# Attention and gated MLP on one core: q and k stacks moved per head, one transfer for the reciprocals, pairs ordered at the score buffers, another start order

## The chip, the cores and the metric

The kernel runs on one core of a Trainium2 chip. The metric is device time in microseconds of one launch. Three runs of the kernel before gave 1013.47, 1013.8 and 1016.6, so the median is 1013.8 us. The profile comes from a separate execution of 1009.12 us, whose span from first to last instruction is 1007.3 us.

## The reference, cut to what matters

```
q, k, v: 8 batches x 8 heads x 576 positions x 64
q, k = rotate(q), rotate(k)              # rotary embedding, x*cos + swapped(x)*sin
attn = softmax(q k^T / 8), 576 x 576     # max subtracted, sum + 1e-9
x    = attn v, heads side by side        # 8 x 576 x 512
h    = relu(x w_in)                      # 512 -> 1024, halves u and v
v_n  = (v - mean) / sqrt(var + 1e-6)
v_s  = w_spatial v_n + b_spatial         # mixes the 576 positions
out  = (u * v_s) w_out                   # 512 -> 512
```

All arithmetic is to float32 accuracy. A matmul operand is split into a rounded high part and a low rest, and products of parts are summed: three matmuls per product in the MLP; in the scores the high and the low half of a factor are stacked on the 128 rows, so two matmuls do.

## The kernel before, in words

**Pairs and batches.** The unit of attention is a pair of heads; there are 4 pairs per batch and 32 in all. After the four pairs of a batch comes that batch's MLP.

**One pair.** `prepare(i)` (L440) loads q and k into two stage buffers `st` (three slots), multiplies by the rotation tables and adds (L485, L489, mostly GpSimd), rounds the high parts (`hq` by L368, high k in the second half of `st[1]` by L501) and takes the rests (`lq` L371, `lk` L469). Eleven DMAs on SP's queue then build the operands of the score matmuls: `ks` (4: each head's high k at its own rows and at the other head's rows), `qs` (2 from `hq`, 2 from `lq`) and `qz` (3). `qs`, `ks`, `qz`, `hq` and `lq` exist once each, and `lk` has one slot. So the stacks of pair i+1 may be written only when the scores of pair i have been read out of them.

**Scores.** `scores` (L551) runs nine times per pair, in the order `TILES` = 0, 1, 2, 3, 8, 4, 5, 6, 7: tiles 0 to 3 are head 0, tiles 4 to 7 head 1, tile 8 (fifth in order) holds the last 64 rows of both heads. Each is 4 or 6 matmuls into a score buffer (`sc`, two in PSUM), a row maximum on VectorE (L571), an exponential on ScalarE (L572) into `e` (three slots) and a transpose on VectorE (L582) into `tu` (one slot). `need` (L569) makes every tile wait for all stacks of both heads.

**Values.** `attention` (L523) then multiplies the transposed tiles with v (L541): 288 small matmuls, in three chunks, into two `pm` buffers and one of the two `sc` buffers. `normalise` (L586) inverts the sums (L621, L622), transposes them into `rt` (L623), writes them to a scratch in DRAM by four DMAs (`put`), reads them back spread over the partitions by three (`get`, into `rb`), and multiplies the values by them (L618, L619). Only then is the value accumulators' PSUM, the `sc` buffer among it, free.

**The MLP.** Four products: L660 (v half of h), L683 (u half), L701 (spatial) and L721 / L738 (output), 360 matmuls per batch. Its weights arrive as 64-bit floats and are decoded at the start (`decode`, L376): twelve pieces of 512 KB, each six VectorE and two ScalarE instructions.

**What sets the order.** Every instruction group is an `op` with an estimated duration and a key. `Program.run` (L138) plays the program with these estimates: an engine that is free takes the ready op with the lowest key whose buffers are free. The order that comes out is written into the instruction queues, and each queue runs in that order on the chip, waiting where an estimate was too short. The DMAs of `load` (L365) and `unroll` (L350 to L352) all stand in SP's one queue. Until 100 us of planned time, idle TensorE slots are filled with matmuls on zeros (L795).

Of the kernel before, what the change touches and what calls it, by code (L numbers as in the profile page):

```python
# [8 lines left out]
F32 = mybir.dt.float32  # L9
# [7 lines left out]
P = 128  # L17
# [7 lines left out]
HALF = S // 2  # L25
# [6 lines left out]
TO_PE = 105  # L32
IBUF, BLOCK, FETCH = 544, 256, 3900
SLOTS = {
    "stage": 3, "lk": 1, "vraw": 1, "e": 3, "tu": 1, "rb": 1, "x32": 1, "xg": 7, "m": 4,
    "small": 3, "nmx": 3, "rt": 2, "sc": 2, "pm": 4,
}
PSUM = {"sc": 1024, "pm": 512}
MOE_START, MOE_LENGTH = 163.72, 41.17
DEC_V = [-3.48, -27.9, 65.72, -23.46]  # L40
DEC_S = [83.89, 51.11, 39.65]
DEC_U = [-100.9, 67.61, 53.75, 139.76]
DEC_ON = -44.85
DEC_O = [-11.86, 63.73, 86.56, 156.33]

NB = S // 32
TILES = [0, 1, 2, 3, 8, 4, 5, 6, 7]
NV = 4 * NQ
JC = 4 * P + 16
Q4 = S // 4  # L50
CHUNKS = 3
QE = JC + P
EARLY = 73.59
STEAL = 145.22
WARM_FROM, WARM_FULL, WARM_TO, WARM_NS, WARM_AFTER, WARM_COLS = 2500, 44958.22, 100000, 170, -0.15, 384
PATIENT = (DVE, ACT, POOL)
UNTIL = 144.95
LATE_LOAD = 2200
FIRST = 6
PREP = [-17.58, -1.0, 26.46, -6.17, -39.31, -66.56, -25.92, 107.58]  # L60
PREP_E = [114.39, 49.39, -30.17, 40.83, 35.03, -30.24, -3.45, 80.62]
PREP_AT = [37.74, 27.86, 33.62, 20.81, 13.42, 36.67]
STAGE = [-22.63, 3.68, -25.96, -10.67, -21.35, 14.58, 46.93]
STAGE_E = [-7.1, 1.79, 3.9, 176.64, 8.86, -89.19, 11.72]
ATT_AT = [-190.38, 50.74, 48.75, -18.56, -25.99, -28.18]
NORM = [-24.83, -11.6, 65.82, 18.85, 38.51]
NORM_E = [92.6, -206.08, -98.79, -5.14, -12.64]
MOE0 = [281.73, 20.17]
K_NORM, K_RELU, K_GATE, K_GHI, K_GLO, K_OB, K_OUT = 158.97, -96.57, 62.21, 63.93, -95.55, -267.44, -2.21


def pe_ns(n, m=P):
    return max(m * 5 // 6 + 3, n * 11 // 24)
# [33 lines left out]
class Program:  # L107
# [5 lines left out]
    def op(self, eng, ns, key, f, r=(), w=(), new=(), port=False, late=0):  # L113
        return self.either({eng: ns}, key, lambda e: f(), r, w, new, port, late)
# [23 lines left out]
    def run(self, make, warm):  # L138
# [34 lines left out]
        while events:  # L173
# [29 lines left out]
            for e in LATENCY:  # L203
# [17 lines left out]
                        kept = kept or len(item[2].new) == 3  # L221
                if chosen and e in PATIENT:
                    soon[e] = {a for a in soon[e] if not a.eng and a.due > now}
                    if any(a.key < min(chosen.key, UNTIL) and a.due < now + chosen.costs[e] * 0.5 for a in soon[e]):
                        for b in chosen.new:
                            free[b.pool].insert(0, b.slot)
                            own[b.pools[0]] += 1
                        passed.append(item)
                        chosen = None
                for item in passed:  # L230
                    heapq.heappush(ready[e], item)
                if e == PE and not chosen and max(WARM_FROM, idle + (WARM_AFTER if now > WARM_FULL else 0)) <= now < WARM_TO and free["pm"]:
                    chosen = warm()
                    chosen.bufs[0].pool, chosen.bufs[0].slot = "pm", free["pm"].pop(0)
                    index[chosen] = len(index)
                    left += 1
# [36 lines left out]
def tile_attention_gated_mlp(  # L273
# [24 lines left out]
    def make(b):  # L298
        tag = f"{b.pool}{b.slot}"
        if b.pool in PSUM:  # L300
            return ps.tile([P, PSUM[b.pool]], F32, tag=tag, name=b.name, bufs=1)
        if b.pool == "rt":
            b.scratch = dr.tile([9, P], F32, tag=tag, name=b.name + "d", bufs=1)
        return sb.tile(b.shape, b.dt, tag=tag, name=b.name, bufs=1)

    prog = Program()
# [47 lines left out]
    def at(t, offset, *dims):  # L354

        return bass.AP(tensor=t.tensor, offset=t.offset + offset, ap=[list(d) for d in dims])
# [7 lines left out]
    def load(dst, src):  # L364
        nc.sync.dma_start(out=dst, in_=src)  # L365
# [10 lines left out]
    def decode(key, where, at, src):  # L376
# [26 lines left out]
            return lambda: ts(out=ints(), in0=word(1), scalar1=s1, scalar2=s2, op0=op0, op1=op1)  # L403

        t0, t1 = (tok, 0), (tok, 1)
        op(DMA, 1500, key - 8, fetch, w=[t0, t1])
        op(DVE, 640, key, bits(20, 0x7FF, ALU.logical_shift_right, ALU.bitwise_and), r=[t1], w=[pt], new=[pt])
        op(ACT, 600, key - DEC_ON, lambda: nc.scalar.activation(ints(), ints(), AF.Relu, bias=bias, scale=float(2**23)), r=["bias"], w=[pt])
        op(DVE, 640, key - DEC_ON, lambda: stt(out=sg.tile, in0=word(1), scalar=-(2**31), in1=ints(), op0=ALU.bitwise_and, op1=ALU.bitwise_or), r=[t1, pt], w=[sg], new=[sg])
# [5 lines left out]

    def spatial(key, j):
        st = Buf("xg", [P, 2, S], F32, f"ws{j}")
        op(DMA, 1700, key - 8, lambda: load(st.tile, w_spT[j * P:(j + 2) * P, :].rearrange("(c p) t -> p c t", p=P)), w=[st], new=[st])
        for c in range(2):
            t = ("wsp", j + c)  # L420
            op(ACT, 573, key, lambda c=c: round_hi(wsp[:, j + c, 0, :], st[:, c, :]), r=[st], w=[(t, 0)])
            pair_op(S, key, lambda e, c=c: rest_lo(e, wsp[:, j + c, 1, :], st[:, c, :], wsp[:, j + c, 0, :]), r=[st, (t, 0)], w=[t])
# [17 lines left out]
    def prepare(i):  # L440
# [60 lines left out]
        op(ACT, 573, key - K_HIQ, lambda: nc.scalar.activation(hk(), st[1][:, :S], AF.Copy, scale=0.125), r=[(st[1], 0)], w=[(st[1], 1)])  # L501
        op(DVE, dve_ns(S), key - K_LOK, lo_k, port=True, r=[(st[1], 0), (st[1], 1)], w=[lk], new=[lk])

        def stack(dst, src, swap):
            for a in range(2):
                rows = slice(64 * a, 64 * a + 64)
                to = slice(64 - 64 * a, P - 64 * a) if swap else rows
                load(raw(dst[to, a, :]), raw(src[rows, :]))

        def to_z():  # L510
            load(raw(qz[0:64, :QE]), raw(hq[0:64, :]))
            load(raw(qz[64:P, JC:QE]), raw(hq[64:P, 4 * P:JC + P - 16]))
            load(raw(qz[64:P, QE:]), raw(hq[64:P, :4 * P]))

        op(DMA, 1250, key - K_STACK, lambda: stack(qs, hq, False), r=["hq"], w=[("qs", 0)])
        op(DMA, 1250, key - K_STACK, lambda: stack(ks, hk(), False), r=[(st[1], 1)], w=[("ks", 0)])
        op(DMA, 1250, key - K_STACK2, lambda: stack(ks, hk(), True), r=[(st[1], 1)], w=[("ks", 1)])
        op(DMA, 1850, key - K_STACK, to_z, r=["hq"], w=["qz"])
        op(DMA, 1250, key - K_STACK2, lambda: stack(qs, lq, True), r=["lq"], w=[("qs", 1)])

    raw = lambda t: t.bitcast(F32)

    def attention(i):  # L523
        lk, vr = prepped[i]
        sm = sums[i % 2]
        key = 20 * i
        K_S, K_STEP, K_MAX, K_EXP, K_TURN, K_CHUNK, K_VAL = STAGE_E if i < FIRST else STAGE
        if i < FIRST:
            key += ATT_AT[i]
        tu = Buf("tu", [P, NB, HALF], F32, f"tu{i}")  # L530
        for n, c in enumerate(TILES):
            scores(i, c, lk, sm, key + K_S + K_STEP * n, K_MAX, K_EXP, K_TURN, tu, n == 0)
        pv = [*[Buf("pm", None, None, f"pv{i}_{g}") for g in range(2)], Buf("sc", None, None, f"pv{i}_2")]

        def values(n):
            outs = [pv[0][:, :Q4], pv[1][:, :Q4], pv[2][:, :Q4], pv[2][:, 512:512 + Q4]]
            for kb in range(NB * n // CHUNKS, NB * (n + 1) // CHUNKS):
                for a in range(2):
                    for g in range(4):
                        rows = slice(32 * g, 32 * g + 32)  # L540
                        nc.tensor.matmul(outs[g][64 * a:64 * a + 64], lhsT=vr[rows, NQ * (kb % 4) + kb // 4, a, :], rhs=tu[rows, kb, Q4 * a:Q4 * a + Q4], start=(kb == 0), stop=(kb == NB - 1), tile_position=(32 * g, 64 * a))  # L541

        for n in range(CHUNKS):
            o = op(PE, NB * 243 // CHUNKS + 200, key + K_VAL + K_CHUNK * n, lambda n=n: values(n), r=[vr, *[(tu, c) for c in TILES]], w=pv, new=pv if n == 0 else [])
            o.words = NB * 32 // CHUNKS
        normalise(i, sm, pv, key)

# [3 lines left out]
    def scores(i, c, lk, sm, key, k_max, k_exp, k_turn, tu, first):  # L551
# [14 lines left out]
                for n_c in range(2):  # L566
                    nc.tensor.matmul(pt[:, n_c * 512:n_c * 512 + HALF], lhsT=lhsT, rhs=rhs[:, n_c * HALF:n_c * HALF + HALF], start=(n == 0), stop=(n == len(parts) - 1))  # L567

        need = [lk, ("qs", 0), ("qs", 1), ("ks", 0), ("ks", 1), "qz"]  # L569
        op(PE, (6 if c == 8 else 4) * pe_ns(HALF), key, mm, r=need, w=[pt], new=[pt])  # L570
        op(DVE, 749, key + k_max, lambda: nc.vector.tensor_reduce(out=nmx.tile, in_=tops(pt), op=ALU.max, axis=AX.XY, negate=True), r=[pt], w=[nmx], new=[nmx])  # L571
        op(ACT, 920, key + k_exp, lambda: nc.scalar.activation(e.tile.rearrange("p (c n) -> p c n", c=2), tops(pt), AF.Exp, bias=nmx.tile, scale=1.0, accum_out=sm[:, col:col + 1]), r=[pt, nmx], w=[e, ("sums", i % 2, c)], new=[e])  # L572

# [12 lines left out]
    def normalise(i, sm, pv, key):  # L586
# [6 lines left out]
        need = [("sums", i % 2, c) for c in range(9)]  # L593

        def put():
            for g in range(4):
                load(at(rt.scratch, 9 * 32 * g, (32, 9), (1, 32)), rt[32 * g:32 * g + 9, :])

        def get():
            load(rb[0:64], at(rt.scratch, 0, (0, 64), (9 * 32, 4), (1, Q4)))  # L600
            load(rb[64:P, :, :P], at(rt.scratch, P + 32, (0, 64), (9 * 32, 4), (1, P)))
            load(rb[64:P, :, P:], at(rt.scratch, Q4, (0, 64), (9 * 32, 4), (1, 16)))

        def low(e):
            rest_lo(e, four(x[:, S + TW:S + TW + 4 * P]), x32[:, :, :P], four(x[:, :4 * P]))
# [15 lines left out]
        op(ACT, 100, key + K_INV, lambda: nc.scalar.activation(sm[:, 0:9], sm[:, 0:9], AF.Copy, bias=1e-9), w=need)  # L621
        op(DVE, 130, key + K_INV, lambda: nc.vector.reciprocal(out=sm[:, 0:9], in_=sm[:, 0:9]), w=need)  # L622
        op(DVE, 125, key + K_INV, lambda: nc.vector.transpose(out=rt.tile, in_=sm), r=need, w=[rt], new=[rt])  # L623
        op(DMA, 1500, key + K_INV, put, r=[rt], w=[(rt, 1)], late=2000)
        op(DMA, 1850, key + K_GET, get, r=[(rt, 1)], w=[rb], new=[rb], late=1000)
        op(DVE, dve_ns(S) + 220, key + K_X, scale, r=[*pv, rb], w=[x32], new=[x32])
        op(ACT, 660, key + K_XHI, high, r=[x32, *([("gated", i // NP - 1)] if i >= NP and i % NP == NP - 1 else [])], w=[(x, 0)], new=[x])
# [172 lines left out]
    pairs = [(b, hp) for b in range(B) for hp in range(NP)]  # L800
    prepped, xs = [], []
    n_setup = [("sums", n, c) for n in range(2) for c in range(9)]
    n_setup += [("qs", 0), ("qs", 1), "qz", "hq", "lq"]
    op(POOL, 2000, -126, setup, w=["bias", *n_setup])

    def tables():
# [85 lines left out]
```

## Time and profile before

| | |
|---|---|
| median of three runs | 1013.8 us |
| profiled execution | 1009.12 us |
| its span | 1007.3 us |
| mean granted TensorE clock | 0.944 of full speed |
| TensorE busy | 894.8 us (89%), of which 74.8 us on zeros |
| VectorE / ScalarE / GpSimd busy | 608.8 / 490.8 / 482.9 us |
| moved by DMA | 160.78 MB, mean 160 GB/s |

Busy shares are averages over a start (weights are loaded and decoded, no MLP yet), a long middle (attention of one batch beside the MLP of the batch before) and an end (the last MLP alone). TensorE's busy time counts modelled matmul ends and matmuls at the low clock, so it is more than the work would take at full speed.

### The profile page before, as it was taken

Reading aid. Unit: us, or ns where it says so; the run is one execution under the profiler, and the core shown is the slowest. Engines: PE = TensorE matmul, PEld = TensorE weight load, DVE = VectorE, ACT = ScalarE, POOL = GpSimd, SP = SyncE. Lnnn points to the kernel's source line nnn. Section 1 sums busy time; section 2 is a strip of 40 time slices with the busy share of each in tenths; the row PEclk is TensorE's granted clock in tenths of the full one; section 3 lists DMA queues with packets and bytes.
Section 4 is the critical chain, followed back from the end, with each engine's and each line's share of the span. In section 5 each row is a group of like instructions: output and inputs, shape, how many; then the busy total and the mean of one; then the engine's idle time right before and its main releaser. Section 6 shows DMA issues by size and latency. Waiting matters only on the chain.

```text
span 1007.3 us, 32514 instructions
## 1 busy us (share of the span) xinstructions
PE 894.8 (89%) x13677; PEld 784.3 (78%) x13677; DVE 608.8 (60%) x1202; ACT 490.8 (49%) x1207; POOL 482.9 (48%) x468
## 2 busy tenths in 40 slices
PE   8779856989898999989799997998899987999998
PEld 4456645788788887888778986887779886898898
DVE  3888865645677654745576665655576645765331
ACT  1454433644456543654456453753456443663352
POOL 3554344454555561845356654545356651742022
PEclk9789957989999999999989997999989998999999
DMA  9976666755777668766686677775676667855101
GB/s 242 258 210 182 156 146 130 176 145 131 168 199 162 159 153 212 179 157 152 165 190 152 159 199 164 168 169 138 172 179 141 164 167 184 192 130 124 62 1 48
DMA packets 99380, 160.78 MB, mean 160 GB/s; under 512 B 26849, under 2 KB 45665, under 8 KB 99234
## 3 DMA queue, kind: packets, MB, share of 16 engines
q1 hardware_dynamic: 98578, 157.45, 64.8%
q8 instruction: 108, 1.77, 0.8%
q10 hardware_dynamic: 656, 1.25, 0.5%
q14 instruction: 38, 0.31, 0.1%
HBM read 98.08 MB, written 9.58 MB: 107 GB/s over the span
## 4 chain that ended last, share of the span: by engine, by line
PE 40%; SPq 10%; DMA 6%; issue 4%; DVE 4%; POOL 2%; ACT 2%; DVEq 0%; POOLq 0%
PE sc L567 9%; SPq L365 7%; PE pc L701 7%; PE pb L683 7%; PE pd L721 6%; PE pv L541 6%; PE pa L660 5%; DMA st<-in_qk_dram 2%; POOL st L485 1%; DVE tu L582 1%; SPq L352 1%; SPq L351 1%; POOL st L489 1%; DMA ks<-st 1%; SPq L350 1%
## 5 line engine op out<-in xcount | busy, mean ns | idle before, releaser
L571 DVE TENSOR_REDUCE nmx<-sc 128x1 f32<-128x576 f32 x288 | 212.8, 747 | 197.6 <-PE sc L567 194.8
L572 ACT ACTIVATE e<-sc,nmx 128x576 f32<-128x576 f32 x288 | 212.7, 740 | 172.8 <-DVE nmx L571 170.8
L582 DVE STREAM_TRANSPOSE tu<-e 128x576 f32<-128x576 f32 x288 | 219.0, 767 | 42.8 <-ACT e L572 33.4
L485 POOL TENSOR_TENSOR st<-st,tabs 128x576 f32<-128x576 f32 x124 | 175.0, 1433 | 109.2 <-DMA st<-in_qk_dram 102.7
L541 PE MATMUL pv<-tu,vr 32*64 32x144 f32 x9216 | 187.7, 294 | 33.6 <-issue 20.4
L567 PE MATMUL sc<-ks,qs 128*128 128x288 f32 x640 | 153.2, 332 | 62.1 <-ACT e L572 30.4
L541 PEld LDWEIGHTS pv<-tu,vr 32*64 32x64 f32 x9216 | 155.7, 134 | 61.8 <-issue 43.5
L567 PEld LDWEIGHTS sc<-ks,qs 128*128 128x128 f32 x640 | 110.7, 205 | 85.4 <-ACT e L572 38.1
L567 PE MATMUL sc<-lk,qz 128*128 128x288 f32 x576 | 132.3, 313 | 0.0
L371 POOL TENSOR_TENSOR lq<-st,hq 128x512 fp32r<-128x512 f32 (+1 forms) x62 | 48.5, 807 | 169.8 <-ACT hq L368 168.0
L660 PE MATMUL pa<-wi,x 128*128 128x512 f32 x448 | 122.4, 410 | 0.1
L701 PE MATMUL pc<-wsp,vn 128*128 128x288 f32 x768 | 121.7, 297 | 0.0
L683 PE MATMUL pb<-x,wi 128*128 128x288 f32 x768 | 115.8, 296 | 0.3 <-ACT vv L759 0.3
L721 PE MATMUL pd<-g,wo 128*128 128x288 f32 x744 | 113.5, 300 | 0.0
L683 PEld LDWEIGHTS pb<-x,wi 128*128 128x128 f32 x768 | 106.6, 188 | 4.7 <-issue 1.8
L701 PEld LDWEIGHTS pc<-wsp,vn 128*128 128x128 f32 x768 | 108.0, 188 | 2.8 <-issue 2.8
L721 PEld LDWEIGHTS pd<-g,wo 128*128 128x128 f32 x744 | 104.7, 192 | 1.8 <-issue 1.8
L567 PEld LDWEIGHTS sc<-lk,qz 128*128 128x128 f32 x576 | 100.9, 205 | 0.1
L660 PEld LDWEIGHTS pa<-wi,x 128*128 128x128 f32 x448 | 83.0, 196 | 17.6 <-issue 3.7
L489 POOL TENSOR_TENSOR st<-st 128x576 f32<-128x576 f32 x62 | 89.2, 1439 | 4.9 <-DVE st L485 2.0
L371 POOL TENSOR_TENSOR x<-x,x 128x64 fp32r<-128x64 f32 (+1 forms) x96 | 59.3, 647 | 67.1 <-ACT x L368 67.1
L795 PE MATMUL warm<-zero 128*128 128x384 bf16 x365 | 74.8, 348 | 13.0 <-DVE wi L371 10.1
(104 smaller groups left out, 772.4 us busy)
## 6 DMA issues: line engine op xcount, KB each, us to landing
vr<-in_v_dram SPq DMA_DIRECT2D x128, 320.0 KB
st<-in_qk_dram SPq DMA_DIRECT2D x32, 576.0 KB
ks<-st SPq DMA_DIRECT2D x128, 144.0 KB
qs<-lq SPq DMA_DIRECT2D x64, 164.0 KB
qs<-hq SPq DMA_DIRECT2D x64, 164.0 KB
st<-in_qk_dram SPq DMA_DIRECT2D x32, 288.0 KB
out_dram<-ob SPq DMA_DIRECT2D x31, 288.0 KB
st<-in_qk_dram SPq DMA_DIRECT2D x32, 256.0 KB
```

The lines of the kernel that those rows point to most:

```text
L371: eng.tensor_tensor(out=lo, in0=src, in1=hi.bitcast(F32), op=ALU.subtract)
L485: f = lambda e: e.tensor_tensor(out=st[j][:, cols], in0=st[j][:, cols], in1=tabs[j][:, cols], op=ALU.mult)
L489: f = lambda e: e.tensor_tensor(out=st[j][:, :S], in0=st[j][:, :S], in1=st[j][:, S:2 * S], op=ALU.add)
L541: nc.tensor.matmul(outs[g][64 * a:64 * a + 64], lhsT=vr[rows, NQ * (kb % 4) + kb // 4, a, :], rhs=tu[rows, kb, Q4 * a:Q4 * a + Q4], start= ...
L567: nc.tensor.matmul(pt[:, n_c * 512:n_c * 512 + HALF], lhsT=lhsT, rhs=rhs[:, n_c * HALF:n_c * HALF + HALF], start=(n == 0), stop=(n == len( ...
L571: op(DVE, 749, key + k_max, lambda: nc.vector.tensor_reduce(out=nmx.tile, in_=tops(pt), op=ALU.max, axis=AX.XY, negate=True), r=[pt], w=[n ...
L572: op(ACT, 920, key + k_exp, lambda: nc.scalar.activation(e.tile.rearrange("p (c n) -> p c n", c=2), tops(pt), AF.Exp, bias=nmx.tile, scale ...
L582: nc.vector.transpose(out=dst, in_=src)
L660: nc.tensor.matmul(pm[:, :HF], lhsT=lhsT, rhs=win[1, d][:, j, :], start=(d == 0 and n == 0), stop=(d == 3 and n == len(todo) - 1))
L683: nc.tensor.matmul(pm[:, :HALF], lhsT=win[0, d][:, i, f * P:(f + 1) * P], rhs=x[d][:, at:at + HALF], start=(d == 0 and n == 0), stop=(d == ...
L701: nc.tensor.matmul(pm[:, :HALF], lhsT=lhsT, rhs=rhs, start=(t == 0 and n == 0), stop=(t == 4 and n == 1))
L721: nc.tensor.matmul(pm[:, :HALF], lhsT=wout[d,][:, i, m * P:(m + 1) * P], rhs=gs[d][:, at:at + HALF], start=(d == 0 and n == 0), stop=(d == ...
```

## The change

The moves of the stacks are grouped by head rather than by operand. The same eleven DMAs are issued, but the tokens are per head (`("ks", a)`, `("qs", a, 0)`, `("qs", a, 1)`, `("qz", a)`), and a score tile waits only for the stacks of the heads that it reads. `lk` gets a second slot.

Two ordering tokens are added for the planner. `("all", i - 1)`: no score tile of pair i is placed before the last of pair i-1. `("go", i - 1)`: tiles after the fourth of pair i are not placed before the first value chunk of pair i-1. Zero matmuls are not placed while values wait for their buffers.

`put` becomes one DMA of the whole 128x32 tile, into a scratch of that shape, and `get` reads it with the matching strides.

The estimated durations of some DMAs change (weight pieces 1500 to 2200, spatial loads 1700 to 2300, `put` 1500 to 600), and nearly all keys change: the order of the decoding, the keys of `prepare`, `scores`, `normalise` and the MLP. `UNTIL` and the factor `SOON` change when VectorE, ScalarE and GpSimd hold back for a more urgent op.

```diff
-    "stage": 3, "lk": 1, "vraw": 1, "e": 3, "tu": 1, "rb": 1, "x32": 1, "xg": 7, "m": 4,
+    "stage": 3, "lk": 2, "vraw": 1, "e": 3, "tu": 1, "rb": 1, "x32": 1, "xg": 7, "m": 4,
-MOE_START, MOE_LENGTH = 163.72, 41.17
-DEC_V = [-3.48, -27.9, 65.72, -23.46]
-DEC_S = [83.89, 51.11, 39.65]
-DEC_U = [-100.9, 67.61, 53.75, 139.76]
+MOE_START, MOE_LENGTH = 92.6, 82.21
+DEC_V = [-26.92, 52.32, 24.86, 22.99]
+DEC_S = [150.62, 151.46, 121.54]
+DEC_U = [13.26, 87.85, 110.17, 61.84]
-PREP_E = [114.39, 49.39, -30.17, 40.83, 35.03, -30.24, -3.45, 80.62]
-PREP_AT = [37.74, 27.86, 33.62, 20.81, 13.42, 36.67]
-STAGE = [-22.63, 3.68, -25.96, -10.67, -21.35, 14.58, 46.93]
+PREP_E = [56.57, 104.31, -2.68, 90.22, 41.0, 15.18, 35.33, 70.53]
+PREP_AT = [-49.94, 1.99, -17.86, 1.88, 5.93, 3.81]
+STAGE = [-8.68, 1.44, -30.59, -19.57, 31.94, 1.12, 13.88]
-MOE0 = [281.73, 20.17]
+MOE0 = [84.13, 114.68]
...
-            b.scratch = dr.tile([9, P], F32, tag=tag, name=b.name + "d", bufs=1)
+            b.scratch = dr.tile([P, 32], F32, tag=tag, name=b.name + "d", bufs=1)
...
-        op(DMA, 1250, key - K_STACK, lambda: stack(qs, hq, False), r=["hq"], w=[("qs", 0)])
-        op(DMA, 1250, key - K_STACK, lambda: stack(ks, hk(), False), r=[(st[1], 1)], w=[("ks", 0)])
-        op(DMA, 1250, key - K_STACK2, lambda: stack(ks, hk(), True), r=[(st[1], 1)], w=[("ks", 1)])
-        op(DMA, 1850, key - K_STACK, to_z, r=["hq"], w=["qz"])
-        op(DMA, 1250, key - K_STACK2, lambda: stack(qs, lq, True), r=["lq"], w=[("qs", 1)])
+        def high_q(a):
+            own, _ = half(a)
+            load(raw(qs[own, a, :]), raw(hq[own]))
+            if a == 0:
+                load(raw(qz[own, :QE]), raw(hq[own]))
+            else:
+                load(raw(qz[own, JC:QE]), raw(hq[own, 4 * P:JC + P - 16]))
+                load(raw(qz[own, QE:]), raw(hq[own, :4 * P]))
+
+        def high_k(a):
+            own, other = half(a)
+            load(raw(ks[own, a, :]), raw(hk(own)))
+            load(raw(ks[other, a, :]), raw(hk(own)))
+
+        def low_q(a):
+            own, other = half(a)
+            load(raw(qs[other, a, :]), raw(lq[own]))
+
+        for a in range(2):
+            late = K_LATE * a
+            op(DMA, 1250, key - K_STACK + late, lambda a=a: high_k(a), r=[(st[1], 1)], w=[("ks", a)])
+            op(DMA, 1250 + 600 * a, key - K_STACK + late, lambda a=a: high_q(a), r=["hq"], w=[("qs", a, 0), ("qz", a)])
+            op(DMA, 650, key - K_STACK2 + late, lambda a=a: low_q(a), r=["lq"], w=[("qs", a, 1)])
...
-            o = op(PE, NB * 243 // CHUNKS + 200, key + K_VAL + K_CHUNK * n, lambda n=n: values(n), r=[vr, *[(tu, c) for c in TILES]], w=pv, new=pv if n == 0 else [])
+            o = op(PE, NB * 243 // CHUNKS + 200, key + K_VAL + K_CHUNK * n, lambda n=n: values(n), r=[vr, *[(tu, c) for c in TILES]], w=[*pv, *[("go", i)][:1 - n]], new=pv if n == 0 else [])
...
-        need = [lk, ("qs", 0), ("qs", 1), ("ks", 0), ("ks", 1), "qz"]
-        op(PE, (6 if c == 8 else 4) * pe_ns(HALF), key, mm, r=need, w=[pt], new=[pt])
+        need = [lk, *[t for a in heads for t in (("qs", a, 0), ("qs", a, 1), ("ks", a), ("qz", a))]]
+        op(PE, (6 if c == 8 else 4) * pe_ns(HALF), key, mm, r=[*need, ("all", i - 1), *([("go", i - 1)] if TILES.index(c) > SLOTS["e"] else [])], w=[pt, *([("all", i)] if c == TILES[-1] else [])], new=[pt])
...
         def put():
-            for g in range(4):
-                load(at(rt.scratch, 9 * 32 * g, (32, 9), (1, 32)), rt[32 * g:32 * g + 9, :])
+            load(rt.scratch, rt.tile)
```

## Rows read from the trace of the kernel before

**Rows 1.** Stages: stretch, length, busy PE, PEld, DVE, ACT, POOL; clock, DMA share, GB/s.
```profile
43.60:170.40 126.80, 95.88 (x1535) 70.69 (x1535) 93.23 (x151) 53.54 (x123) 57.59 (x54) 0.83 0.73 183
294.40:941.00 646.60, 590.71 (x9616) 537.36 (x9615) 400.44 (x814) 338.49 (x850) 330.87 (x317) 0.96 0.69 163
```

**Rows 2.** Sums turned for the reciprocals, once per pair: first and last start.
```profile
L623 DVE STREAM_TRANSPOSE rt<-sums x32: 169/204/214, 59.4 to 941.1; 128x32 f32<-128x32 f32 x32
...
L365 SPq DMA_DIRECT2D rt3d<-rt x4: 304/310/450, 151.6 to 152.8; - x4
```

**Rows 3.** SP's queue in time: start us, us, operation, count. Stacks of pair 19.
```profile
565.03 7.80 SPq L365 DMA_DIRECT2D ks<-st  x2
...
576.78 1.54 SPq L365 DMA_DIRECT2D rt18d<-rt  x4
578.37 2.21 SPq L365 DMA_DIRECT2D qz<-hq  x3
...
583.91 1.91 SPq L365 DMA_DIRECT2D rb<-rt18d  x3
```

**Rows 4.** TensorE in time, same stretch: last tile of pair 18, tiles of 19.
```profile
572.14 0.43 PE L567 MATMUL sc<-lk,qz 128*128 128x288 f32 x2
...
583.49 0.53 PE L567 MATMUL sc<-ks,qs 128*128 128x288 f32 x2
...
586.13 0.43 PE L567 MATMUL sc<-ks,qs 128*128 128x288 f32 x2
...
599.05 0.43 PE L567 MATMUL sc<-lk,qz 128*128 128x288 f32 x2
```

**Rows 5.** VectorE in time, pair 18: last transpose and its normalisation.
```profile
575.24 0.78 DVE L582 STREAM_TRANSPOSE tu<-e 128x576 f32<-128x576 f32 x1
...
587.91 0.52 DVE L618 TENSOR_TENSOR x<-pv,rb 128x144 f32<-128x144 f32 x2 [0.30 <-DMA rb<-rt18d]
```

**Rows 6.** Who SP's queue waited for: us in total, times, longest.
```profile
SPq L365 <- PE sc L567: 272.7, 55, 7.5
```

**Rows 7.** Pieces of the chain that ended last: start us, us, what.
```profile
564.73 1.33 PE sc L567 x10
...
941.63 1.71 PE pv L541 x96
...
950.36 11.74 PE pa L660 x50
...
964.69 10.53 PE pb L683 x78
...
977.60 13.69 PE pc L701 x103
991.29 9.18 PE pd L721 x69
```

**Rows 8.** Idle time of TensorE, whole span: line, releaser, us, times, longest.
```profile
PEld pv L541 <- issue: 43.5, 97, 2.1
...
PE pv L541 <- issue: 20.4, 23, 1.9
```

**Rows 9.** Idle time of TensorE from 170 to 950 us, same columns.
```profile
PE sc L567 <- DVE x L619: 23.7, 15, 3.1
```

**Rows 10.** SP's queue at the start: pair 0's first and last stack moves.
```profile
19.28 1.90 SPq L365 DMA_DIRECT2D ks<-st  x2
...
36.77 1.75 SPq L365 DMA_DIRECT2D qz<-hq  x3
```

**Rows 11.** TensorE in time: the first score matmul.
```profile
43.61 0.51 PE L567 MATMUL sc<-ks,qs 128*128 128x288 f32 x2
```

**Rows 12.** Costly groups: busy us, mean ns of one, idle before.
```profile
L571 DVE TENSOR_REDUCE nmx<-sc 128x1 f32<-128x576 f32 x288 | 212.8, 747 | 197.6 <-PE sc L567 194.8
L582 DVE STREAM_TRANSPOSE tu<-e 128x576 f32<-128x576 f32 x288 | 219.0, 767 | 42.8 <-ACT e L572 33.4 <-PE pv L541 8.3
...
L412 DVE SCALAR_TENSOR_TENSOR dcwi<-dcwi,sgwi 128x512 f32<-128x512 f32 x8 | 5.6, 696 | 0.2
```

## What the change was expected to do

> **What bounds the kernel now.** I read the busy time by stages first. In the middle, TensorE is busy 590.7 of 646.6 us at 0.96 of full clock [rows 1], which looks like an engine near its limit. The length of a pair says otherwise. The sums of a pair are turned once per pair, from 59.4 to 941.1 us [rows 2]: 31 periods of 28.4 us; those up to pair 3 take 30.7 us each, when no MLP runs yet, the 28 after it 28.2 us. A period that is the longer without the MLP's work is no TensorE limit.
>
> What TensorE needs per pair, at full clock, comes from pieces of the last chain [rows 7]. Scores: 38 matmuls at 0.133 us = 5.05. Values: 288 at 1.71/96 = 0.0178 us = 5.13. MLP per batch: 56 at 11.74/50 = 0.235, 96 at 10.53/78 = 0.135, 112 at 13.69/103 and 96 at 9.18/69 = 0.133: 53.8 us, so 13.4 per pair. Together 23.6 us, 4.6 less than the period.
>
> The ring is seen in SP's queue and TensorE read side by side. Pair 18's last score matmul ends at 572.57 [rows 4]. Only then can SP issue the stacks of pair 19: its `ks` entry ends at 572.83 after a wait, the last `qz` is issued at 580.58, with four puts of 1.54 us in between [rows 3]. The first score of pair 19 starts at 583.49 and its last ends at 599.48 [rows 4]. So a period is a gap of 10.9 us (8.0 of issues, 2.9 until the last has landed) and a score stage of 16.0 us (1.78 per tile). SP waits 272.7 us in all for score matmuls [rows 6], 8.8 per pair. In the gap TensorE has values and MLP work, but the gap makes the MLP of a batch run out before the next batch's inputs are there, and this is where idle time and low clock come from.
>
> **The change part by part.** *Stacks by head.* The eleven DMAs stay, at (8.0 - 1.54)/11 = 0.59 us of issue each. Head 0's five can go once the fifth tile of the pair before has been computed: 2.9 us of issue and 2.9 of landing, 5.8 us, beside four head-1 tiles that take 4 x 1.78 = 7.1 us. They are hidden, with 1.3 us to spare. Head 1's six need 3.5 + 2.9 = 6.4 us after the last tile; the first tile that wants them is the fifth of the next pair, behind four head-0 tiles and a value chunk. Hidden too. If that cover fails, the fifth tile waits up to the old gap. `lk`'s second slot adds no instruction; without it the next pair could not start beside the old one.
>
> What is late next is the ring through `tu`, of one slot. After the last transpose ends (576.02, [rows 5]) the values run until 583.49 [rows 4]: 7.5 us with MLP matmuls in between. Three tiles of the next pair can wait in the three `e` slots; six remain: 6 x 1.78 = 10.7 us. From the last score to the last transpose it is 576.02 - 572.57 = 3.45 us. Sum 21.6 us. Lower end: values alone 3 x 1.71 = 5.1 [rows 7], tiles at VectorE's own pace, 0.747 + 0.767 = 1.51 us [rows 12]: 5.1 + 9.1 + 3.45 = 17.7. Upper end: no tile runs ahead, 7.5 + 16.0 + 3.45 = 27.0. I take 21.6, as the code now lets three tiles through ahead of the values.
>
> So TensorE becomes the bound: 23.6 us, plus what it waits for its own instructions, 43.5 + 20.4 = 63.9 us over 32 pairs [rows 8], 2.0 per pair, which no edit removes, plus 0.8 for score tiles that wait for a buffer held by the values until they are scaled (23.7 us in 28 periods, [rows 9]). That is 26.4 us. Bounds: 23.6 with all of this hidden, 28.2 as now. The clock's loss (0.96 in the middle, 0.9 us per period) I count as gone with the idle stretches; it is inside the bounds.
>
> *Reciprocals in one transfer.* Three issues less, 3/4 of 1.54 = 1.2 us of SP per pair. The way from the turned sums to the scaled values is 576.0 to 587.9, 11.7 us [rows 5]; it gets 1.2 us shorter, inside the 0.8 above, so I add nothing. The transfer carries 16 KB in place of 4.6 KB; landing could be longer or shorter by some tenths, against a get that starts 5.6 us after the puts (578.32 to 583.91, [rows 3]).
>
> *Order of pairs.* Both new tokens join matmuls of one engine and cost no wait of their own; they fix the order in TensorE's queue. Behind a value chunk that waits for the last transpose stand the tiles from the fifth on and MLP matmuls. Cost between nothing and the 2 us per pair by which a value chunk may be planned too early; I take nothing, MLP work being keyed evenly over the next four pairs to fill.
>
> *SP's queue.* It waits twice per pair for scores in place of once. Behind each wait stand puts, gets, the q, k and v loads and output stores. The 8.8 us of waiting per pair show the room; gain or loss here is in the rivals.
>
> *Start.* Pair 0's first stack moves are issued at 19.28 us, its last at 36.77 to 38.52, behind weight and spatial loads [rows 10]; the first score starts at 43.61 [rows 11]. The new keys put pair 0's stacks (-85 and -120) ahead of all weight pieces but those already issued (-35 and up). Eleven issues from 19.3 end at 25.8; landing took 5.1 us there: 30.9 at best, 43.6 at worst. I take 34, nearer to the row, for loads already queued. The sums of pair 0 then turn 15.8 us later (59.4 - 43.6), at 50. The three periods up to pair 3 have no MLP: 21.6 us for the ring, but VectorE also decodes. Twelve pieces of six instructions at 0.696 us [rows 12] are 50 us, and from 43.6 to 170.4 it is busy 93.2 of 126.8 us [rows 1]. With some 32 us of decoding left for four pairs, 8 us each and half of it in the ring's way (an estimate), I take 26, between 21.6 and the 30.7 of now. Pair 3 then turns at 50 + 78 = 128 us in place of 151.
>
> *Sum.* 128 + 28 x 26.4 + 66.2 for the end after pair 31 (1007.3 - 941.1, the last MLP on TensorE alone, unchanged) = 933.4 us of span. The profiled execution is 1.8 us longer than its span and 4.7 us under the median of the runs: 933.4 + 1.8 + 4.7 = 940 us.
>
> **The rivals.** *Another ring takes over.* No tile runs ahead, since the order planned on estimates does not come true and the values sit between the pairs: 27.0 us from above and the buffer waits of 0.6 left, 27.6 from pair 0 on: 50 + 31 x 27.6 + 66.2 = 972, about 978 us. For it: one slot of `tu`, one of two score buffers lent to the values. Against it: three `e` slots. That the split moves nothing forward belongs here: with the whole gap left but for 1.2 us of puts the period is 27.0.
>
> A rule speaks for that. The Trainium skill, "DMA: Bandwidth & Descriptors", section "Rules for kernel authors", says that two transfers to disjoint partition halves are not worth splitting, as both spread over the same 16 engines and serialise. The trace does not bear it out as the limit: the engines are 0.69 busy in the middle [rows 1], and only 2.9 of the gap's 10.9 us is landing; the split is to start earlier, not to go faster.
>
> *Faster than forecast.* Instruction waits are partly filled by interleaved MLP matmuls and the ring stays at its lower end: 25.0 us, and 23 in the start: 50 + 69 + 700 + 66.2 = 885, about 892 us. For it: 23.6 us of bare work. Against it: two value chunks now follow each other closely, which is where these waits fall [rows 8].
>
> *Slower than before: SP's queue blocks the reciprocals.* If the get of pair i stands behind the wait for the fifth tile of pair i+1, the values keep their score buffer, and tiles go at the one-buffer pace, 583.49 to 586.13, 2.64 us [rows 4]. The `tu` ring is then 7.5 + 6 x 2.64 + 3.45 = 26.8, and head 1's stacks, queued behind the get, add their landing of 2.9: 29.7 us. 50 + 31 x 29.7 + 66.2 = 1037, about 1043 us. It decides from a mean period of (1007.3 - 66.2 - 50)/31 = 28.7 us. For it: one queue in planned order. Against it: the get's key (+90) and the head-1 stacks (about +62 for the next pair) are both ready soon after the last tile, well before that fifth tile.
>
> **How the numbers follow.** The forecast, with a period of 25.5 to 27.2 us (915 to 962 us), gets 0.55; another ring 0.20; faster than forecast 0.12; slower 0.10; no change 0.03, where every gain is eaten by new waits. Within 0.3% is about what a measurement of this kernel can tell from no change. Faster: 0.55 + 0.20 + 0.12 = 0.87. The range of 890 to 1000 us reaches over both fast rivals and leaves out the slower one, no change and the outer edges.
>
> **What would show it.** Right: the turned sums come every 26 to 27 us; the time from one pair's last score to the next pair's first falls from 10.9 to under 4 us; SP's `ks` entries come in twos, twice per pair; pair 3's sums at 120 to 135 us; middle clock near 1.0. Wrong: a period at 28 with the gap moved in front of the fifth tile (stacks too late) or in front of the first transpose (values late), gets issued over 8 us after the puts, or a first score still after 40 us.

## The result, and the profile after

The changed kernel takes 938.08 us (median of four runs, 936.52 to 940.61); the kernel before took 1013.63 us beside it. The ratio is 0.9261, 95% interval 0.9219 to 0.9303. The forecast was 940 us. The number came out nearly exact; three of its terms did not, and they cancelled.

Of the pages, the chain that ended last in the kernel before, then the span and that chain in the changed kernel:

```profile
PE 40%; SPq 10%; DMA 6%; issue 4%; DVE 4%; POOL 2%; ACT 2%; DVEq 0%; POOLq 0%
```
```profile
span 938.8 us, 32216 instructions
...
PE 68%; DMA 18%; DVE 5%; issue 4%; SPq 3%; ACT 1%; ACTq 0%; DVEq 0%
```

Stages of the changed kernel: stretch, length, then busy time of TensorE's matmuls and weight loads, VectorE, ScalarE and GpSimd, clock, DMA share, GB/s.

```profile
43.60:131.00 87.40, 71.06 (x1105) 47.90 (x1102) 67.33 (x114) 36.82 (x85) 32.98 (x32) 0.82 0.81 194
...
240.00:856.00 616.00, 592.18 (x9970) 540.10 (x9969) 412.98 (x841) 347.72 (x882) 344.03 (x329) 0.99 0.77 182
```

The middle's clock went from 0.96 [rows 1] to 0.99, its DMA share from 0.69 to 0.77: nearly the same bytes (160.78 and 161.13 MB in all) in less time.

The turned sums, once per pair, and SP's put of pair 3 (compare [rows 2]):

```profile
L634 DVE STREAM_TRANSPOSE rt<-sums x32: 189/202/213, 46.6 to 859.4; 128x32 f32<-128x32 f32 x32
...
L367 SPq DMA_DIRECT2D rt3d<-rt x1: 332/332/332, 139.3 to 139.3; - x1
```

From pair 3's put to pair 31's turn a period is (859.4 - 139.3)/28 = 25.7 us, 28.2 before. The three periods before that are (139.3 - 46.6)/3 = 30.9 us, 30.7 before: the start got no faster pace. The put stands in for the turn of pair 3's sums here, as in the prediction. In the kernel before it was issued 3.0 us after that turn; VectorE in time, before and then after:

```profile
148.60 0.21 DVE L623 STREAM_TRANSPOSE rt<-sums 128x32 f32<-128x32 f32 x1
```
```profile
139.03 0.20 DVE L634 STREAM_TRANSPOSE rt<-sums 128x32 f32<-128x32 f32 x1
```

By the turns alone the later periods went from 28.3 to 25.7 us, and the three first ones from 29.7 to 30.8. After the last sums come 938.8 - 859.4 = 79.4 us, 66.2 before.

SP's queue in time, head 0 of pair 20 and then head 1 of it (compare [rows 3]):

```profile
541.20 0.51 SPq L367 DMA_DIRECT2D qs<-lq  x1
541.75 1.25 SPq L367 DMA_DIRECT2D ks<-st  x2
543.04 0.62 SPq L367 DMA_DIRECT2D qs<-hq  x1
543.76 0.54 SPq L367 DMA_DIRECT2D qz<-hq  x1
548.00 0.46 SPq L367 DMA_DIRECT2D qs<-lq  x1
...
551.02 1.24 SPq L367 DMA_DIRECT2D qz<-hq  x2
...
554.68 0.59 SPq L367 DMA_DIRECT2D rt19d<-rt  x1
...
558.26 1.92 SPq L367 DMA_DIRECT2D rb<-rt19d  x3
```

TensorE in the same stretch (compare [rows 4]): the fifth tile of pair 19, its last tile, then the first tile of pair 20, value chunks of pair 19, and the fifth tile of pair 20.

```profile
540.64 0.68 PE L579 MATMUL sc<-ks,qs 128*128 128x288 f32 x4
541.16 0.43 PE L579 MATMUL sc<-lk,qz 128*128 128x288 f32 x2
...
547.81 0.43 PE L579 MATMUL sc<-lk,qz 128*128 128x288 f32 x2
...
551.00 0.43 PE L579 MATMUL sc<-ks,qs 128*128 128x288 f32 x2
...
554.01 1.78 PE L553 MATMUL pv<-tu,vr 32*64 32x144 f32 x96
...
560.34 1.78 PE L553 MATMUL pv<-tu,vr 32*64 32x144 f32 x96
...
565.17 0.81 PE L579 MATMUL sc<-ks,qs 128*128 128x288 f32 x4 [0.88 <-DVE x L630]
```

Head 0's moves are issued from 541.20 on, as the fifth tile ends, and head 1's from 548.00 on, as the last tile ends (548.24). The first tile of pair 20 follows 2.8 us after that, where 10.9 us passed before [rows 4]. Four tiles of pair 20 run before or between the value chunks: three fill the `e` slots, the fourth waits in a score buffer.

For all pairs I take the starts of the 288 row maxima (L583; L571 before), nine to a pair. From the last of a pair to the first of the next it is 3.8 us on average over pairs 6 to 31; before it was 11.8. From a pair's first to its fifth it is 15.2 us; before 9.9. So 8.0 us went and 5.3 came back, 3.6 of them between the fourth and the fifth tile (5.8 us, before 2.2): the values now sit there.

SP's waits for score matmuls fell from 272.7 us [rows 6] to 123.6, and a wait for the values came up:

```profile
SPq L367 <- PE sc L579: 123.6, 58, 6.7
SPq L367 <- PE pv L553: 98.7, 28, 7.1
```

### The profile page after: what moved, and what is told of

Its sections match the earlier page's. It is cut to its first block, busy times and chain, and to the rows that moved or that the text cites. A ratio compares the mean times of both kernels' runs of the same rounds, so it can differ in the third digit from the quotient of the medians.

```text
span 938.8 us, 32216 instructions
## 1 busy us (share of the span) xinstructions
PE 864.5 (92%) x13594; PEld 762.6 (81%) x13594; DVE 599.9 (64%) x1203; ACT 484.7 (52%) x1207; POOL 483.1 (51%) x467
## 2 busy tenths in 40 slices
DMA packets 101682, 161.13 MB, mean 172 GB/s; under 512 B 29153, under 2 KB 47969, under 8 KB 101538
## 4 chain that ended last, share of the span: by engine, by line
PE 68%; DMA 18%; DVE 5%; issue 4%; SPq 3%; ACT 1%; ACTq 0%; DVEq 0%
PE sc L579 15%; PE pv L553 14%; PE pc L712 10%; PE pb L694 9%; PE pd L732 9%; PE pa L671 8%; PE warm L806 3%; DMA qz<-hq 3%; DMA qs<-hq 3%; SPq L367 3%; DMA vr<-in_v_dram 1%; DVE tu L594 1%; DVE nmx L583 1%; DMA ks<-st 1%; DMA wi10raw<-in_w_in_dram 1%
## 5 line engine op out<-in xcount | busy, mean ns | idle before, releaser
L583 DVE TENSOR_REDUCE nmx<-sc 128x1 f32<-128x576 f32 x288 | 212.8, 744 | 153.6 <-PE sc L579 146.4
L594 DVE STREAM_TRANSPOSE tu<-e 128x576 f32<-128x576 f32 x288 | 213.8, 759 | 35.0 <-PE pv L553 28.9
L553 PE MATMUL pv<-tu,vr 32*64 32x144 f32 x9216 | 182.9, 291 | 25.9 <-issue 25.0
L553 PEld LDWEIGHTS pv<-tu,vr 32*64 32x64 f32 x9216 | 150.5, 132 | 50.8 <-issue 46.1
L579 PE MATMUL sc<-ks,qs 128*128 128x288 f32 x640 | 145.1, 317 | 40.9 <-DVE x L630 15.8
L579 PE MATMUL sc<-lk,qz 128*128 128x288 f32 x576 | 129.2, 307 | 1.5 <-DMA qz<-hq 1.3
L712 PE MATMUL pc<-wsp,vn 128*128 128x288 f32 x768 | 125.2, 298 | 0.2 <-ACT u L697 0.2
L694 PE MATMUL pb<-x,wi 128*128 128x288 f32 x768 | 119.8, 300 | 0.1
L579 PEld LDWEIGHTS sc<-lk,qz 128*128 128x128 f32 x576 | 96.4, 197 | 3.5 <-DMA qz<-hq 3.3
L671 PEld LDWEIGHTS pa<-wi,x 128*128 128x128 f32 x448 | 79.5, 189 | 16.3 <-issue 4.0
L373 POOL TENSOR_TENSOR g<-u,g 128x288 fp32r<-128x288 f32 x64 | 52.7, 824 | 75.2 <-ACT g L370 75.1
## 6 DMA issues: line engine op xcount, KB each, us to landing
st<-in_qk_dram SPq DMA_DIRECT2D x32, 576.0 KB, 4.5
```

The costliest lines, as they stand in the source:

```text
L373: eng.tensor_tensor(out=lo, in0=src, in1=hi.bitcast(F32), op=ALU.subtract)
L594: nc.vector.transpose(out=dst, in_=src)
L671: nc.tensor.matmul(pm[:, :HF], lhsT=lhsT, rhs=win[1, d][:, j, :], start=(d == 0 and n == 0), stop=(d == 3 and n == len(todo) - 1))
L694: nc.tensor.matmul(pm[:, :HALF], lhsT=win[0, d][:, i, f * P:(f + 1) * P], rhs=x[d][:, at:at + HALF], start=(d == 0 and n == 0), stop=(d == ...
L712: nc.tensor.matmul(pm[:, :HALF], lhsT=lhsT, rhs=rhs, start=(t == 0 and n == 0), stop=(t == 4 and n == 1))
```

## The experiments

The period in this section is the time from pair 3's put to pair 31's turned sums, over 28; the gap is the one from row maximum to row maximum, over pairs 6 to 31. Except in experiments 9 and 10, every edit also made the planner order the queues anew.

**1. All tiles wait for both heads.**

```diff
-        need = [lk, *[t for a in heads for t in (("qs", a, 0), ...
+        need = [lk, *[t for a in range(2) for t in (("qs", a, 0), ...
```

> The changed kernel, but every score tile waits for the stacks of both heads. Theory (the gap between a pair's last and the next pair's first score was what the change removed): all eleven moves stand behind the last tile again, 11 x 0.59 us of issue and 2.9 of landing, a gap of over 8 us; the period goes from 25.7 back to 27 to 28.5 us and the time to 975 to 1015 us. Rival (the new keys made the gain, the split is incidental): the time stays within 930 to 955 us.

Measured: 1036.72 us, ratio 1.0223 to before (1.0156 to 1.0290). Period 29.5 us, gap 12.1 us. Turned sums, and then the last tile of pair 16, the last stack issue and the first tile of pair 17:

```profile
L634 DVE STREAM_TRANSPOSE rt<-sums x32: 194/211/214, 49.3 to 969.1; 128x32 f32<-128x32 f32 x32
```
```profile
521.89 0.43 PE L579 MATMUL sc<-lk,qz 128*128 128x288 f32 x2
...
534.07 0.53 PE L579 MATMUL sc<-ks,qs 128*128 128x288 f32 x2
```
```profile
527.61 1.66 SPq L367 DMA_DIRECT2D qz<-hq  x2
```

The old gap is back, 522.3 to 534.1, with the keys and all else unchanged in the code. The direction holds; it costs more than I expected. The new keys are worse than the old ones where the gap stands, as experiment 3 shows too.

**2. New code, old keys.** All keys as before, for instance:

```diff
-MOE_START, MOE_LENGTH = 92.6, 82.21
+MOE_START, MOE_LENGTH = 163.72, 41.17
...
-SOON = 44.64
+SOON = 0.5
...
-STAGE = [-8.68, 1.44, -30.59, -19.57, 31.94, 1.12, 13.88]
+STAGE = [-22.63, 3.68, -25.96, -10.67, -21.35, 14.58, 46.93]
```

> The changed code with all keys of before (start, scores, values, MLP, holding back). Theory (the split alone makes the ring shorter): period 26 to 27 us after pair 3, pair 3 turned near 150 us as before: 151 + 28 x 26.4 + 66 + 6 = 962, say 950 to 985 us. Rival (the split is worth nothing without its keys): 1000 us or more.

Measured: 1010.02 us, ratio 0.9951 (0.9919 to 0.9983). My theory missed. The gap did fall, to 3.2 us, but the period is 27.9: the step from the fourth to the fifth tile is 13.2 us. TensorE in time: fourth tile of pair 18, values of pair 17 from first to last chunk, fifth tile of pair 18.

```profile
545.85 0.43 PE L579 MATMUL sc<-lk,qz 128*128 128x288 f32 x2
546.21 0.46 PE L553 MATMUL pv<-tu,vr 32*64 32x144 f32 x4
...
554.64 1.81 PE L553 MATMUL pv<-tu,vr 32*64 32x144 f32 x96
...
558.90 0.69 PE L579 MATMUL sc<-ks,qs 128*128 128x288 f32 x4
```

The values stand in one block of 10.2 us behind all four tiles that could run ahead, and everything else waits for the one `tu` slot. The price is near that of the rival of another ring, 27.6 us forecast and 27.9 measured, but in that rival no tile was to run ahead; here four do, and the values stand behind them.

**3. Old code, new keys.** The keys of the changed kernel in the kernel before; the same lines the other way, without `SOON`, which that code does not have.

```diff
-STAGE = [-22.63, 3.68, -25.96, -10.67, -21.35, 14.58, 46.93]
+STAGE = [-8.68, 1.44, -30.59, -19.57, 31.94, 1.12, 13.88]
...
```

> The code of before with all keys of the changed kernel. Theory (the ring through the stacks stands whatever the keys): period 28 us or more, only the start earlier: 985 to 1025 us. Rival (keys made the gain): under 970 us.

Measured: 1061.68 us, ratio 1.0460 (1.0379 to 1.0542); period 29.8, gap 12.0. The ring stands; I had not expected the keys to be so much worse without the split.

**4 and 5. Less work for TensorE, planned anew.** In both kernels, one of three products in the u half and the output:

```diff
-                        for n, (i, j) in enumerate(((0, 0), (0, 1), (1, 0))):
+                        for n, (i, j) in enumerate(((0, 0), (0, 1))):
...
-                    key = mm(3 * pe_ns(HALF), mul, ...
+                    key = mm(2 * pe_ns(HALF), mul, ...
```

> The changed kernel without one of the three products in the u half of h (L694) and in the output (L732): 63 of 360 MLP matmuls of a batch are left out, 63 x 0.134 = 8.4 us per batch, 2.1 us per pair. Theory (TensorE now bounds the middle): nearly all of it shows, 45 to 68 us less: 870 to 895 us. Rival (a ring through the tu slot or the score buffers bounds the middle): only the end's 8 us and little else, 920 to 935 us.

Measured: 960.30 us, ratio 0.9477 (0.9407 to 0.9546): slower than the changed kernel by 22 us, with 67 us of matmuls less.

> The kernel before without one of the three products in the u half of h (L683) and in the output (L721): 63 MLP matmuls of a batch left out, 8.4 us per batch. Theory (before, the ring through the stacks was the bound, not TensorE): only the end's 8.4 us and a few more: 992 to 1008 us. Rival (TensorE was the bound already): 45 to 68 us less, 945 to 970 us.

Measured: 1017.74 us, ratio 1.0057 (1.0024 to 1.0089). Neither theory nor rival. The smaller durations gave the planner another order throughout, and that cost more than the cut saved (shown by 10, where the order is kept). Both are inconclusive on the bound and were run again as 9 and 10.

**6. Four puts in the changed kernel.** The scratch, `get`'s strides and the planned 1500 as before, and

```diff
-            load(rt.scratch, rt.tile)
+            for g in range(4):
+                load(at(rt.scratch, 9 * 32 * g, (32, 9), (1, 32)), rt[32 * g:32 * g + 9, :])
```

> The changed kernel with the four puts of before in place of one. Theory (the put's 1.2 us of SP's time lie beside other work, as the prediction priced it at nothing): within 5 us of the changed kernel, 933 to 944 us. Rival (SP's queue or the way of the reciprocals sets the period): 1.2 us or more per pair, 975 us.

Measured: 935.66 us, ratio 0.9261 (0.9201 to 0.9321), the same as the change's. The transfer in one piece is worth nothing that can be measured here, with the reserve that the order is a new one.

**7. One slot of `lk` in the changed kernel.**

```diff
-    "stage": 3, "lk": 2, ...
+    "stage": 3, "lk": 1, ...
```

> The changed kernel with one slot of lk. Theory: lk of the next pair is written only after the last score, 0.7 us on VectorE plus its place in the queue, so no tile runs ahead of it; the values fill part of that time, so the period grows by 0.5 to 2 us: 950 to 995 us. Rival (the second slot is spare): 933 to 944 us.

Measured: 951.10 us, ratio 0.9426 (0.9364 to 0.9488). The gap is 4.8 us (3.8 with two slots). Pair 3's put comes at 145.6 in place of 139.3, and the 28 periods take 724.3 in place of 720.1 us: more is lost in the start than in the middle. The time is where I expected it, but not for the reason: the next pair still starts soon after the old one.

**8. The start's keys alone, in the kernel before.** Decoding, first six pairs, first MLP, for instance:

```diff
...
-PREP_AT = [37.74, 27.86, 33.62, 20.81, 13.42, 36.67]
+PREP_AT = [-49.94, 1.99, -17.86, 1.88, 5.93, 3.81]
...
```

> The kernel before with only the keys of the start (decoding, first six pairs, first MLP) of the changed kernel. Theory: the first score comes near 28 us in place of 43.6 and pair 3's sums near 139 in place of 151, the period after that stays at 28.2: 997 to 1006 us. Rival (the start's order is worth nothing where the ring is the bound anyway): 1008 to 1018 us.

Measured: 1025.74 us, ratio 1.0157 (1.0099 to 1.0215). The first row maximum came at 26.9 us in place of 44.4, but pair 3's put at 160.3 in place of 151.6: what is gained before the first score is lost again within three pairs. Missed.

**9 and 10. The same cut as 4 and 5, order kept.** Only the products are left out; the planned `3 * pe_ns(HALF)` stays, so every queue has the order of the kernel it is compared with; read tile by tile, the traces show it on all engines.

```diff
-                        for n, (i, j) in enumerate(((0, 0), (0, 1), (1, 0))):
+                        for n, (i, j) in enumerate(((0, 0), (0, 1))):
...
```

> The changed kernel without one of the three products in the u half of h (L694) and in the output (L732), but with the planned durations left as they are, so that every queue keeps the order of the changed kernel: 63 matmuls of a batch are left out, 8.4 us per batch, 67 us in all. Theory (TensorE bounds the middle, and the earlier run of this cut was spoilt by another order): 45 to 67 us less than the changed kernel, 870 to 893 us. Rival (a ring bounds the middle too): the end's 8 us and up to 20 more, 908 to 930 us.

Measured: 929.00 us, ratio 0.9152 (0.9079 to 0.9226). The changed kernel stands at 0.9261, so 1.2% came off, some 11 us (the intervals overlap by a hair), of the 67 us of matmuls left out. In the profiled run the 28 periods from pair 3 take 848.1 - 134.4 = 713.7 us, against 720.1; the cut removed 28 x 2.1 = 59 us of work there. That run is the fastest of its four and the changed kernel's profiled run the slowest of its four, so 6.4 us is rather too much than too little. The rival holds. The chain's shares by engine:

```profile
PE 51%; DMA 28%; DVE 7%; issue 5%; SPq 4%; ACT 3%; POOL 1%; ACTq 0%; DVEq 0%
```

The idle time of TensorE, first the changed kernel and then the one with the cut (line, releaser, us, times, longest):

```profile
PE sc L579 <- DMA qs<-hq: 10.8, 4, 4.5
...
PE sc L579 <- ACT e L584: 4.6, 6, 1.8
```
```profile
PE sc L579 <- DMA qs<-hq: 23.3, 12, 4.7
PE sc L579 <- ACT e L584: 12.2, 20, 1.8
```

The work that was taken away turned into waits for the stacks' landing and for the exponentials: TensorE is busy 549.65 of 600 us here.

```profile
240.00:840.00 600.00, 549.65 (x9525) 483.13 (x9526) 401.02 (x826) 337.31 (x864) 339.12 (x322) 0.99 0.78 184
```

> The kernel before with the same cut and the same order of every queue as before. Theory (the ring through the stacks bounds it, TensorE only fills): the end's 8 us and up to 12 more, 992 to 1006 us. Rival (TensorE bounds it as well): 45 to 67 us less, 945 to 968 us.

Measured: 996.69 us, ratio 0.9811 (0.9743 to 0.9878). In the profiled run the end is 8.1 us shorter and 28 periods 4.7 us. As the theory had it.

**11. Experiment 2 with the MLP's keys of the change.**

```diff
-MOE_START, MOE_LENGTH = 163.72, 41.17
+MOE_START, MOE_LENGTH = 92.6, 82.21
```

> The changed code with all keys of before, except that the MLP is keyed over four pairs as in the changed kernel (MOE_START, MOE_LENGTH). Theory (with the old keys the MLP runs in a bunch, the values stand late behind it and the wait moves in front of the fifth tile): most of the missing gain comes back, 955 to 985 us, and the step from the fourth to the fifth tile falls from 13.2 us to under 9. Rival (the keys of scores and values are what is missing): 998 to 1020 us.

Measured: 1096.13 us, ratio 1.0746 (1.0644 to 1.0847); period 31.0, fourth to fifth tile 16.5 us. The theory is wrong: with MLP work spread over all pairs and the values keyed late, the block of values gets longer still.

**12. Experiment 11 with `STAGE` of the change too**, the keys of scores, maxima, exponentials, transposes and values.

```diff
-STAGE = [-22.63, 3.68, -25.96, -10.67, -21.35, 14.58, 46.93]
+STAGE = [-8.68, 1.44, -30.59, -19.57, 31.94, 1.12, 13.88]
```

> The changed code with all keys of before, except MOE_START, MOE_LENGTH and STAGE (keys of scores, maxima, exponentials, transposes and values) of the changed kernel. Theory (MLP spread and values keyed right behind their scores are all that the split needs): 945 to 975 us, period under 26.5. Rival (the keys of preparing, normalising and the start are needed as well): 985 us or more.

Measured: 967.30 us, ratio 0.9516 (0.9453 to 0.9579); period 26.1, fourth to fifth tile 6.2 us.

```profile
L634 DVE STREAM_TRANSPOSE rt<-sums x32: 165/203/213, 57.4 to 885.3; 128x32 f32<-128x32 f32 x32
```

These two sets of keys take the ratio from 0.9951 (experiment 2) to 0.9516; the change is at 0.9261. The 0.0255 left are 26 us, of which 10.8 are the later first sums (57.4 against 46.6 us). The theory named 945 to 975 us and a period under 26.5, and both came true, but the keys of the start are not worthless beside it. `STAGE` alone with the other old keys, and the changed kernel without the new tokens, were not run, so what the tokens are worth is not known.

## Why the prediction was right

**The ring through the stacks.** Right, and shown from both sides: the gap falls from 11.8 to 3.8 us with the split, comes back to 12.1 when the tokens are joined (experiment 1), and stands at 12.0 with all new keys on the old code (experiment 3).

**The split alone.** The forecast counted the order of values and tiles at nothing and put its failure into a rival at 0.20. Experiments 2, 11 and 12 show that this order decides. The new code with the old keys is worth 0.5%, the new keys on the old code lose 4.6%, and together they win 7.4%. The part of the keys that matters in the middle is the one that puts value chunks between the tiles that run ahead, and MLP work evenly beside them.

**TensorE becomes the bound.** This step failed. Its sum, 26.4 us, stands near the measured 25.7, and TensorE is busy 592.18 of 616 us, but experiment 9 takes 2.1 us of work out of every period and gets 0.2 us. The sum also counts one wait twice: in the trace all 20.4 us of the matmuls' idle time at `issue` [rows 8] lie within the 43.5 us of the weight loads', so that term is 0.6 to 1.4 us per pair, not 2.0, and the sum 25.0 to 25.8. The Trainium skill, "Perfetto Trace Analysis", section "Identifying the Most-Contended Engine", warns that matmul occupancy is a poor measure of headroom and points to the share of peak arithmetic and to the weight loads. Here matmuls are busy 96% of the middle and weight loads 540.10 of 616 us, 88%. Experiment 9 agrees that the 96% did not make TensorE the bound.

What bounds the middle is two chains that meet at the fifth tile. The first runs from the fifth tile over head 0's stacks to the next pair's first tile: the fifth tile ends at 541.59 and the next pair starts at 551.00, 9.4 us. The forecast had 5.8 us there, hidden behind 7.1 us of tiles. The issue was as forecast (541.20 to 544.30, 3.1 us, against 2.9); the landing was mis-sized. I had read 2.9 us from the last issue to the first score; here it is 6.7 (544.30 to 551.00). Over pairs 6 to 31 head 0's last move lands 6.2 us after its issue ends, and the first score starts 0.3 us after that. The moves of `qs`, from issue to landing, in the changed kernel and then in experiment 1, where all moves stand in the gap again:

```profile
DMA to landing us min/median/max: 2.4/5.5/9.7
```
```profile
DMA to landing us min/median/max: 2.5/3.0/10.7
```

So moves that were brought forward land later; in experiments 2, 7 and 12, each in another order, the median is 5.6, 5.4 and 5.3. In pair 20 four loads of v, issued from 538.39 to 541.10, stand right ahead of them in SP's queue; that these are the reason no run shows.

The second is the ring through `tu`: a pair's tiles past the fourth wait until the values of the pair before are done. The forecast had this ring at 21.6 us; over pairs 6 to 31 it takes as long as the period. The term that was too small is the values: 7.5 us from the last transpose to their end, measured 11.3 (2.2 until the first, which in TensorE's queue stands behind the next pair's first tile, and 9.1 from first to last). The fifth tile then starts 2.2 us later, and not for `tu` alone: it also needs the score buffer that the values hold until they are scaled. In 8 of the 26 pairs the scaling waited 0.9 to 4.1 us past the values for the reciprocals, with the fifth tile right behind it. Pair 20 is one of them; VectorE in time:

```profile
564.14 0.52 DVE L629 TENSOR_TENSOR x<-pv,rb 128x144 f32<-128x144 f32 x2 [1.19 <-DMA rb<-rt19d]
```

In row maxima, 10.3 us pass from a pair's fifth to the next pair's first, and 15.2 from there to its fifth; together they are the period. With the cut of experiment 9 the same two stretches take 10.3 and 15.0 us, so the work that went was beside them. That these two chains are the bound is read from the traces; neither was shortened by itself to prove it.

**The start.** The first score came at 26.39 us, earlier than the 34 forecast; but the three periods to pair 3 take 30.9 us, not 26. TensorE in time, first score and the values of pair 0:

```profile
26.39 0.82 PE L579 MATMUL sc<-ks,qs 128*128 128x288 f32 x2 [8.25 <-DMA qs<-lq]
...
46.34 2.57 PE L553 MATMUL pv<-tu,vr 32*64 32x144 f32 x139
50.80 1.20 PE L553 MATMUL pv<-tu,vr 32*64 32x144 f32 x53 [1.89 <-issue]
...
56.55 1.25 PE L553 MATMUL pv<-tu,vr 32*64 32x144 f32 x26 [2.44 <-issue]
```

The values, with one tile between them, take 11.5 us in place of the 5.1 that they need; for 4.3 us of it TensorE stands at `issue`, held by nothing that the profile shows. The forecast had this wait at 2 us per pair, an average over the span. That the loads of the start cause it is not shown: they keep the DMA engines 0.95 busy up to 43.6 us, but while these values run the share is 0.65 (columns as above):

```profile
46.30:57.80 11.50, 7.17 (x294) 5.87 (x293) 7.49 (x13) 3.84 (x8) 5.18 (x5) 0.94 0.65 161
```

These 6.4 us are less than half of the 14.7 by which the three periods are longer than forecast; the rest is not traced to a cause. The start also varies from execution to execution: in experiment 9 TensorE's instructions are the same up to 180 us, and pair 3's put comes at 134.4 in place of 139.3. Experiment 8 agrees that an earlier first score does not last. The forecast's own reading of the start was off as well: 151.6 us is pair 3's put, and by its turn at 148.60 a period there took 29.7 us, not 30.7, which is still more than the 28.3 after it.

**The end.** The forecast took 66.2 us over unchanged; it is 79.4. The chain that ended last (start us, us, what), after and then before:

```profile
869.33 12.51 PE pd L732 x93
881.84 11.56 PE pa L671 x50
```
```profile
943.34 0.59 PE pd L721 x3
...
946.15 0.59 PE pd L721 x3
```

The first row is the output product of the MLP of batch 6. Of that MLP 113 matmuls are left after pair 31's turned sums, 8 in the kernel before: 13.2 us of the middle's gain are given back at the end. The MLP's new keys do not explain it. Experiment 2, with the old ones, has 127 left and an end of 80.2 us; experiments 1 and 3, with the new ones and the old gap, have 13 and 20 left and ends of 64.6 and 66.8 us. Among the kernels with all products the late end goes with the closed gap, in which TensorE may have found room for this work; only experiment 11, at a period of 31.0 us, has a closed gap and an end of 64.8 us. The cause is not shown further.

**The sum.** First sums 3.4 us earlier than forecast, start periods 14.7 longer, 28 periods 19 shorter, end 13.2 longer: 5.4 us in the span, 938.8 against 933.4. The right time is partly luck.

**Puts and SP's queue.** Priced at nothing, and experiment 6 shows nothing, though the reciprocals do come last in 8 of 26 pairs, as said above. (From 576.0 to 587.9 it is 11.9 us, not 11.7; no sum uses it.) The slower rival did not come: the get of pair 19 is issued 3.6 us after its put (554.68 to 558.26), before the fifth tile.

## What to carry to other kernels

When buffers exist once, ask for every reader which part of them it needs: half a buffer that is released four tiles earlier took a gap of 11.8 us to 3.8, though the transfers landed later, not sooner. Then look at what stands in the next ring, because the wait moves there unless the order of the work around it moves too. And an engine that is busy 96% is shown to be the bound only when work is taken from it with the order kept.

## What the runs showed of the hardware and the planner that was not expected

The order alone is worth tens of microseconds. The same cut of the same kernel gave ratios of 0.9477 with a new order and 0.9152 with the old one; in the kernel before, 1.0057 and 0.9811: 25 to 33 us. So differences of up to 20 to 30 us between kernels that were planned anew, as experiments 7 and 8 against theirs, are not proof of what the edited part is worth; nor are the equality in experiment 6 and the 0.5% of experiment 2. Those of experiments 1, 3 and 11 are larger, and so are the 43 us between experiments 2 and 12.

Moves of 164 KB within the core took 2.4 to 9.7 us to land, 5.5 at the median, at a DMA share of 0.77; in experiment 1 the median was 3.0 at a share of 0.68. The Trainium skill, "DMA: Bandwidth & Descriptors", section "Rules for kernel authors", says that two transfers to disjoint partition halves serialise. No run here tests that, as the same eleven moves are issued in both kernels. The gain is in when they may start.
